# Ten of thirty-six token tiles: the second feed-forward product as seven half products a pair, joint row statistics, buffers by number, and a new order of all steps

## The chip, the cores and the metric

The kernel runs on one core of a Trainium2 chip. The metric is the device time of one launch in microseconds (us). The core has TensorE (PE in the profile, its weight loads PEld), VectorE (DVE), ScalarE (ACT), GpSimd (POOL) and SyncE (SP), which issues every transfer here.

## The reference

Linear attention, eight batches of eight heads over 576 positions of 64 values, followed by a feed-forward block with a normalised SoLU:

```
q_s = softmax(q, over the 64 values)      k_s = softmax(k, over the 576 positions)
kv  = k_s^T v          (64 x 64 for each head)
x   = q_s kv           -> 4608 tokens x 512
h   = x @ w_in         -> 4608 x 1024
sm  = softmax(h);  solu = h * sm
ln  = (solu - mean) / sqrt(var + 1e-6) * g_ln
out = ln @ w_out       -> 4608 x 512
```

Everything is float32 in and out; the feed-forward weights arrive as float64 words.

## The kernel before, in words

The 4608 tokens are 36 tiles of 128: four (batch, c) tiles for each batch, and one tile for the 64 left-over rows of each two batches. Tiles are numbered 0 to 35 in the order of the batches; 26 and 34 are the left-over tiles of batches 4/5 and 6/7.

A float32 product is made on TensorE from float16 halves: each operand is split into a high and a low part, and high times high, low times high and high times low are summed, three 128-deep matmuls where one would do. The first four tiles use float32 matmuls instead (L775), since the split weights aren't ready yet.

For a tile the steps are: keys and queries softmax (`keys`, `queries`), attention (`attend`, L645), the first product h = x w_in (L783, 24 matmuls 512 wide), the row statistics and the split `u` of the SoLU value (`hidden`, L791 to L854), a transposing transfer of `u` into `uT` (L831), and the second product (`project`, L872): 24 matmuls with 512 columns of moving weights `wo`, stationary operand `uT`, into one PSUM bank. The last tile (35) has its product in two column halves, 24 matmuls 256 wide each. Then ScalarE or VectorE multiplies by the row factor (L885, L883) and SP stores the rows (L888).

From batch 3 on the first product is made for tiles in pairs (`hidden_twin`, L713): two tiles times the two halves of the contraction times two halves of the columns is a 2 x 2 block product, done with seven half products instead of eight, from sums and differences of blocks (`combined` for x, `weights_combined`, step T, for the weights). The statistics of each tile still run by themselves in `hidden`: row maximum, exponential with its sum (L797), the power on GpSimd for the reciprocal (L807), the SoLU value (L814), mean, split, squares (L836), the power for the root (L854).

Nothing is scheduled at run time. `ORDER` is a string of step names; `in_turns` advances one Python generator for each name, and each `yield` ends a step. The instructions thus go into each engine's queue in exactly this order, and each queue runs in order. A suffix .v puts a step on VectorE instead of its own engine. K, Q, V are the steps of a batch's keys, queries and values, x attention, w and y the input and output weights, W and Z their scaling, h, H, o the hidden steps, paired first products and second products, S and R scales and left-over queries, P four idle matmuls ("warm-up", L935).

Buffers of SBUF come from pools that rotate by tag (`uT` 12, `e` 3, `u` 3, `xT` 3, ...); PSUM has three banks `att`, one bank `o` (the last six tiles use both) and two 2-bank slots `h`.

Of the kernel before, what the change touches and what calls it, by code (L numbers as in the profile page):

```python
# [1002 lines left out]
```

## Time and profile before

| what | value |
|---|---|
| three runs, median (lowest to highest) | 443.63 us (443.26 to 443.71) |
| profiled execution, span first to last instruction | 442.6 us |
| TensorE busy | 422.5 us, 95% |
| VectorE / ScalarE / GpSimd busy | 353.7 / 316.8 / 277.2 us |
| DMA | 73.98 MB, mean 167 GB/s |

The profiled execution's own time is known as its span, 442.6 us; the median of the runs is 1.0 us above it. The shares of busy time are means over stages: the first 60 us load and split the weights and the first keys, the middle has all engines full, and in the last 35 us hardly anything but the second product is left.

### The profile page before, as it was taken

Reading aid. Unit: us, or ns where it says so; the run is one execution under the profiler, and the core shown is the slowest. Engines: PE = TensorE matmul, PEld = TensorE weight load, DVE = VectorE, ACT = ScalarE, POOL = GpSimd, SP = SyncE. Lnnn points to the kernel's source line nnn. Section 1 sums busy time; section 2 is a strip of 40 time slices with the busy share of each in tenths; the row PEclk is TensorE's granted clock in tenths of the full one; section 3 lists DMA queues with packets and bytes.
Section 4 is the critical chain, followed back from the end, with each engine's and each line's share of the span. In section 5 each row is a group of like instructions: output and inputs, shape, how many; then the busy total and the mean of one; then the engine's idle time right before and its main releaser. Section 6 shows DMA issues by size and latency. Waiting matters only on the chain.

```text
span 442.6 us, 8818 instructions
## 1 busy us (share of the span) xinstructions
PE 422.5 (95%) x3285; PEld 202.8 (46%) x3285; DVE 353.7 (80%) x740; ACT 316.8 (72%) x549; POOL 277.2 (63%) x330
## 2 busy tenths in 40 slices
PE   2698899999999999999999999999999999999996
PEld 1443344454454444444544445444454444444444
DVE  5999999999998999969988788897776869554431
ACT  2799998696885768778875667588885869683420
POOL 4206974789998768949966988739854464541220
PEclk9999999999999999999999999999999999999999
DMA  8999788579999786478995658966074481635333
GB/s 276 407 309 318 140 154 229 103 210 202 209 208 213 177 131 138 115 201 216 199 246 126 168 100 215 210 170 145 1 169 77 95 189 22 144 71 118 84 99 81
DMA packets 167083, 73.98 MB, mean 167 GB/s; under 512 B 146424, under 2 KB 155904, under 8 KB 167040
## 3 DMA queue, kind: packets, MB, share of 16 engines
q1 hardware_dynamic: 167040, 73.42, 70.5%
q8 instruction: 26, 0.43, 0.4%
q14 instruction: 17, 0.14, 0.1%
HBM read 36.70 MB, written 9.44 MB: 104 GB/s over the span
## 4 chain that ended last, share of the span: by engine, by line
PE 87%; DVE 7%; ACT 2%; issue 1%; DMA 1%; POOL 1%; DVEq 0%; ACTq 0%
PE o L872 42%; PE h L713 22%; PE h L783 12%; PE kv L450 4%; PE x L645 4%; PE h L775 2%; DMA qm<-in_q_dram 1%; DVE iw L265 1%; DVE top L791 1%; DVE gw L265 1%; PE warm_up L935 1%; ACT wi L292 0%; DVE gw L263 0%; DVE qsum L507 0%; DVE qnmx L500 0%
## 5 line engine op out<-in xcount | busy, mean ns | idle before, releaser
L872 PE MATMUL o<-wo,uT 128*128 128x512 f16 (+1 forms) x888 | 195.3, 373 | 0.0
L872 PEld LDWEIGHTS <-uT 128*128 128x128 f16 x888 | 86.1, 98 | 98.8 <-issue 1.8
L783 PE MATMUL h<-wi,xT 128*128 128x512 f16 x240 | 54.4, 379 | 0.0
L713 PE MATMUL h<-wt,split 128*128 128x512 f16 x198 | 46.0, 379 | 0.0
L885 ACT ACTIVATE os<-o,rr 128x512 f32<-128x512 f32 (+1 forms) x28 | 19.0, 678 | 30.6 <-PE o L872 26.8
L713 PEld LDWEIGHTS <-split 128*128 128x128 f16 x264 | 25.8, 98 | 31.5 <-issue 0.7
L436 POOL TENSOR_TENSOR km<-km,kb 128x1152 f32<-128x1152 f32 x13 | 36.7, 2832 | 4.7 <-ACT kb L414 3.2
L824 POOL TENSOR_TENSOR u<-e,u 128x1024 f16<-128x1024 f32 x12 | 26.3, 2191 | 20.0 <-ACT u L151 14.9
L783 PEld LDWEIGHTS <-xT 128*128 128x128 f16 x240 | 23.0, 98 | 27.6 <-issue 0.6
L797 ACT ACTIVATE e<-h,nm,hs 128x1024 f32<-128x1024 f32 x28 | 33.7, 1202 | 0.7
L854 POOL TENSOR_TENSOR r<-var,mhalf 128x1 f32<-128x1 f32 x36 | 22.3, 621 | 17.7 <-DVE var L846 16.9
L527 POOL TENSOR_TENSOR qhl<-qm,qhl 128x512 f16<-128x512 f32 x24 | 28.1, 1189 | 7.6 <-ACT qhl L151 7.0
L814 DVE SCALAR_TENSOR_TENSOR e<-h,ph,e 128x1024 f32<-128x1024 f32 x22 | 28.1, 1280 | 4.3 <-POOL ph L810 2.8
L807 POOL TENSOR_TENSOR p<-pi,mone 128x1 f32<-128x1 f32 x36 | 22.5, 626 | 14.0 <-DVE pi L804 12.5
L713 PE MATMUL h<-wi,xT 128*128 128x512 f16 x132 | 31.0, 379 | 0.0
L775 PE MATMUL h<-iw,xT 128*128 128x512 f32 x64 | 29.4, 602 | 1.2 <-ACT e L838 1.2
L713 PEld LDWEIGHTS <-xT 128*128 128x128 f16 x198 | 19.0, 98 | 22.7 <-issue 0.6
L502 POOL TENSOR_TENSOR qm<-qm,qnmx 128x1024 f32<-128x1024 f32 (+1 forms) x14 | 25.7, 1839 | 5.7 <-DVE qnmx L500 5.7
L520 POOL TENSOR_TENSOR qm<-qm,qrec 128x1024 f32<-128x1024 f32 x12 | 24.3, 2028 | 7.0 <-DVE qrec L511 6.9
L836 ACT ACTIVATE e<-e 128x1024 f32<-128x1024 f32 x22 | 23.2, 1056 | 3.7 <-DVE u L824 3.6
L801 POOL TENSOR_SCALAR am<-top 128x1 f32<-128x1 f32 x22 | 8.3, 376 | 27.9 <-DVE top L746 12.9
L820 ACT ACTIVATE e<-e,nmu 128x1024 f32<-128x1024 f32 x22 | 25.3, 1149 | 0.3
(209 smaller groups left out, 835.3 us busy)
## 6 DMA issues: line engine op xcount, KB each, us to landing
km<-in_k_dram SPq DMA_DIRECT2D x7, 1152.0 KB, 7.5
vm<-in_v_dram SPq DMA_DIRECT2D x28, 288.0 KB, 4.3
out_dram<-os SPq DMA_DIRECT2D x31, 256.0 KB, 3.0
qm<-in_q_dram SPq DMA_DIRECT2D x7, 1024.0 KB, 6.8
wo<-in_moe_w_in_dram SPq DMA_DIRECT2D x4, 512.0 KB, 9.0
w_in<-in_moe_w_in_dram SPq DMA_DIRECT2D x4, 512.0 KB, 9.3
wo<-in_moe_w_out_dram SPq DMA_DIRECT2D x4, 512.0 KB, 4.3
w_out<-in_moe_w_out_dram SPq DMA_DIRECT2D x4, 512.0 KB, 9.0
```

Source lines behind the costliest of these rows:

```text
L436: on(nc.gpsimd).tensor_tensor(km[:, ns], km[:, ns], wide, op=ALU.subtract)
L502: on(nc.gpsimd).tensor_tensor(x, x, wide(nmx), op=ALU.add)
L520: on(nc.gpsimd).tensor_tensor(x, x, wide(rec), op=ALU.mult)
L527: on(nc.gpsimd).tensor_tensor(lo, y, hi, op=ALU.subtract)
L713: nc.tensor.matmul(out, lefts[left](s, i), right_block(right, r, i), start=(n == 0 and not onto), stop=(n + 1 == len(terms)), skip_group_c ...
L775: nc.tensor.matmul(h[:, ns], xT[:, kc], iw[kc][:, ns], start=(i == 0), stop=(i == NP - 1))
L783: nc.tensor.matmul(h[:, ns], xT[:, t, kc], wi[:, s, kc, ns], start=(i == 0), stop=(i == len(terms) - 1))
L797: nc.scalar.activation(e, h, AF.Exp, bias=nm, scale=hs, accum_out=z)
L814: nc.vector.scalar_tensor_tensor(y, h, ph, e, op0=ALU.mult, op1=ALU.mult, accum_out=s1)
L820: nc.scalar.activation(e, e, AF.Identity, bias=nmu)
L824: on(nc.gpsimd).tensor_tensor(u[:, 1], e, u[:, 0], op=ALU.subtract)
L872: nc.tensor.matmul(o, uT[:, j, f], wo[:, s, f, cols], start=(f == 0 and j == 0 and s == 0), stop=(f == NF - 1 and j == 1))
```

## The change

1. **Second product in seven half products.** For the five tile pairs in `SPLIT_OUT` (27 with 28, 29 with 30, 31 with 32, 33 with 35, 26 with 34; ten tiles) `project` is replaced. Two tiles (rows) by two halves of the 1024 contraction by two halves of the 512 output columns is the same 2 x 2 scheme as in `hidden_twin`. Step U (`hidden_pair`, `split_pair`) forms the sums of the SoLU values and splits them in four parts a, b, c, d, each with its own transposing transfer (three of 2048, one of 1024 columns); step O (`pair_products`) has seven products of 12 matmuls, 256 columns wide, into three PSUM banks x, y, z; step E (`pair_rows`) combines, scales and stores. The weights' sums and differences are made once in step TO (`out_combined`): twelve additions or subtractions on GpSimd or VectorE, four casts on ScalarE.
2. **Joint statistics.** The two tiles of such a pair have their statistics in two columns of one small tile, so each small step runs once a pair; both tiles wait for the maxima of both.
3. **Fixed places.** SBUF buffers of 4 KB a partition are 25 numbered "page" places, PSUM is four "bank" and two "h" places; which buffer gets which place stands in a table, `SLOTS`.
4. **Scales.** The normalisation's constants are folded into the scale columns (`isc` has four), so one small step falls away in the single tiles; the reciprocal may run on VectorE.
5. **Order.** The whole `ORDER` string is new, from the first load on. The number of warm-up steps stays seven (28 matmuls).

```
-BUFS = 12, 3, 2
+BUFS = 25, 2
+SPLIT_OUT = (27, 29, 31, 33, 26)
+SLOTS = {
+    "page": (
+        "0 2 5 1 3 4 6 7 8 9 10 11 12 13 14 15 16 17 18 19 20 21 22 23 24 0 2 3 5 11 12 13 16 17 10 4 20 9 22 21 5 "
...
-    "LQ0 Q0b*3 Q0a P LK0 K0 LQ0 LK0 Q0a V02 V01 Q0b Q0a K0 Q0c V00 V03 Q0b*2 V02 K0 V00 K0*3 V01 Q0a K0 w0 "
+    "LK0*2 P*3 K0 LG K0*5 LQ0 Q0a P*2 K0 Q0a V01 K0*4 LG Q0a V02*2 Q0b Q0b.v LG V00*2 LQ0 K0.v K0 Q0c V03*2 Q0a "
...
+    "U26*2 O33*2 U26*2 E33.v E29 E33 E31*2 O26 o25 O33 E33 E33.v O26*2 E26*4 O26*2 E26 h6 E26 O33 O26 E26*2 E33*3 "
+    "O26 E26*3 h3 "
...
+    def hidden_pair(row_tiles):
...
+        nm = pair("nm2")
+        on(nc.gpsimd).tensor_tensor(nm, tops, col(1), op=ALU.mult)
...
+            nc.scalar.activation(e[i], h[i], AF.Exp, bias=nm[:, i : i + 1], scale=hs, accum_out=z[:, i : i + 1])
...
+        for i in range(2):
+            nc.vector.scalar_tensor_tensor(
+                e[i], h[i], ph[:, i : i + 1], e[i], op0=ALU.mult, op1=ALU.mult, accum_out=nmu[:, i : i + 1]
+            )
...
+    def split_pair(row_tiles, name, e, s2):
...
+            cast(on(nc.scalar), u[:, 0], x)
+            yield
+            on(nc.gpsimd).tensor_tensor(u[:, 1], x, u[:, 0], op=ALU.subtract)
+            yield
+            lefts_of[row_tiles[0], part] = turned(None, u, name, part)
...
+        on(nc.gpsimd).tensor_tensor(sums[:, 0], a21, a22, op=ALU.add)
+        yield
+        on(nc.gpsimd).tensor_tensor(a21, a11, a21, op=ALU.subtract)
...
+    def out_combined():
...
+                x = blocks[i, j] = sb.tile([P, NF // 2, DM // 2], F32, name=f"ob{i}{j}", **place("page", SB))
+                on(nc.gpsimd).tensor_tensor(x, wo[:, 0, rows, cols], wo[:, 1, rows, cols], op=ALU.add)
...
+    def pair_products(row_tiles):
...
+        for acc, left, right in (
+            ("x", "11", "11"), ("y", "s2", "t2"), ("z", "s1", "t1"), ("x", "12", "21"), ("y", "s3", "t3"),
+            ("y", "22", "t4"), ("z", "s4", "22"),
+        ):
...
+            for f in range(NF // 2):
+                for n, (j, s) in enumerate(((0, 0), (1, 0), (0, 1))):
+                    nc.tensor.matmul(
+                        accs[acc], t[:, j, first + f], out_block(right, s, f), start=(f == n == 0 and not onto),
...
+    def pair_rows(row_tiles):
...
+        cast(on(nc.scalar), out_rows[:, 0, left], accs["x"])
+        nc.vector.tensor_tensor(accs["y"], accs["y"], out_rows[:, 0, left], op=ALU.add)
...
+        scaled(1, left, "y")
+        yield
+        stored(1)
+        yield
+        scaled_onto(0)
+        yield
+        stored(0)
```

**The start.** SP's queue before, first rows (`qm` queries, `km` keys, `wi` here the place of the first values, `wo` the words of w_in):

```order
L198 DMA qm_96<-in_q_dram 128x8x128
L228 DMA km_110<-in_k_dram 128x2x576
L198 DMA qm_96<-in_q_dram 128x8x128
L228 DMA km_110<-in_k_dram 128x2x576
L211 DMA wi<-in_v_dram 128x576 x4
L250 DMA wo<-in_moe_w_in_dram 128x1024 x2
```

and after the change:

```order
L250 DMA km_98<-in_k_dram 128x2x576 x2
L351 DMA gl_rows<-in_moe_g_ln_dram 8x128
L220 DMA qm_128<-in_q_dram 128x8x128
L233 DMA wi<-in_v_dram 128x576 x3
L220 DMA qm_128<-in_q_dram 128x8x128
L233 DMA wi<-in_v_dram 128x576
L272 DMA wo<-in_moe_w_in_dram 128x1024 x2
```

Both halves of the keys go first, and the gain vector has moved up to the start; the amount ahead of the weights is the same but for its 4 KB. VectorE's queue before, where the key maxima have just been taken (`col` the turned maxima, `km` minus its maximum, `qn` the normalised queries):

```order
L404 TENSOR_REDUCE col_164<-turned_154 128x4
L153 COPY qT_0_180<-qt_1_134 128x512
L502 TENSOR_TENSOR qm_96<-qm_96,qnmx_2_129 128x8x128
L436 TENSOR_TENSOR km_110<-km_110,kb_173 128x2x576 x2
L507 TENSOR_REDUCE qsum_2_233<-qm_96 128x16
L509 TENSOR_SCALAR qden_2_235<-qsum_2_233 128x16
L511 RECIPROCAL qrec_2_237<-qden_2_235 128x16
L517 TENSOR_TENSOR qn_2_128<-qm_96,qrec_2_237 128x2x4x64
```

and after the change, from the same reduction of the turned maxima on:

```order
L427 TENSOR_REDUCE col_148<-turned_143 128x4
L523 TENSOR_REDUCE qnmx_1_162<-qm_128 128x8
L525 TENSOR_TENSOR qm_128<-qm_128,qnmx_1_162 128x8x64
L356 COPY gl<-turned_gl 128x8
L459 TENSOR_TENSOR km_98<-km_98,kb_155 128x2x576
L523 TENSOR_REDUCE qnmx_2_172<-qm_128 128x16
L530 TENSOR_REDUCE qsum_0_176<-qm_128 128x8
L532 TENSOR_SCALAR qden_0_178<-qsum_0_176 128x8
L534 RECIPROCAL qrec_0_180<-qden_0_178 128x8
L175 COPY vm<-wi 128x9x64
```

One of the two subtractions on the keys has gone to GpSimd, the copy into `qT` to ScalarE and the product `qn` to GpSimd; a copy of values has come. Counted over the whole stretch of VectorE's queue that stands ahead of the first low part of the output weights (L368 before, L391 after): gone are one subtraction on `km`, the copy `qT`, the product `qn`, two of three low parts of `wi` (L294, now later) and two single-column steps; new are one subtraction on half of `qm` (512 wide), one maximum `qnmxr` (512 wide), one copy `vm` (576 wide), one `xT` half (256 wide), two more `bd` (256 wide) and some seven single-column steps. TensorE's queue now begins with twenty warm-up matmuls in a row, ahead of the transposes of the key maxima; before, four stood there.

**The end.** VectorE's queue before, last rows (`e` the SoLU value, `u` its split, `os` the output rows):

```order
L824 TENSOR_TENSOR u_4_5398<-e_4_5347,u_4_5398 128x1024
L883 TENSOR_SCALAR os_20_5470<-o_20_5387,rr_2_5385 128x512
L846 TENSOR_SCALAR var_4_5477<-z_4_5475,s_4_5473 128x1
L883 TENSOR_SCALAR os_40_5530<-o_40_5483,rr_4_5481 128x512
L883 TENSOR_SCALAR os_31_5560<-o_31_5535,rr_3_5455 128x256
```

and after the change (`o_4x`, `o_4y`, `o_4z` the three banks of the pair 26/34):

```order
L1077 TENSOR_SCALAR os_2_5498<-o_2x,rr_2_5496 128x256
L1083 SCALAR_TENSOR_TENSOR os_0_5354<-o_0z,rr_0_5312,os_0_5354 128x256
L1083 SCALAR_TENSOR_TENSOR os_2_5498<-o_2z,rr_2_5496,os_2_5498 128x256
L1077 TENSOR_SCALAR os_2_5498<-o_2y,rr_2_5496 128x256
L1091 TENSOR_TENSOR o_4y<-o_4y,os_4_5623 128x256
L1083 SCALAR_TENSOR_TENSOR os_4_5623<-o_4z,rr_4_5621,os_4_5623 128x256
L1083 SCALAR_TENSOR_TENSOR os_2_5498<-o_2z,rr_2_5496,os_2_5498 128x256
L1083 SCALAR_TENSOR_TENSOR os_4_5623<-o_4z,rr_4_5621,os_4_5623 128x256
```

The last instruction is 256 wide in both. SP's queue ends before with one store of 128 rows by 256 columns behind it; after the change the last pair is that of the left-over tiles, whose rows belong to two batches, and four stores of 64 rows by 512 columns end the queue, two of them behind the last instruction of VectorE.

## Rows read from the trace of the kernel before

**Rows 1.** The profile's page, part 1: busy us, share, instructions by engine.

```profile
PE 422.5 (95%) x3285; PEld 202.8 (46%) x3285; DVE 353.7 (80%) x740; ACT 316.8 (72%) x549; POOL 277.2 (63%) x330
```

**Rows 2.** Windows: length, busy us of PE, PEld, DVE, ACT, POOL; clock, DMA, GB/s.

```profile
0.00:62.60 62.60, 47.29 (x466) 23.95 (x467) 54.97 (x106) 50.78 (x82) 31.56 (x33) 1.00 0.92 277
62.60:340.00 277.40, 276.02 (x2262) 131.51 (x2261) 242.72 (x515) 210.86 (x371) 209.74 (x239) 1.00 0.75 166
340.00:439.10 99.10, 99.07 (x561) 47.39 (x559) 55.49 (x120) 55.15 (x98) 35.91 (x60) 1.00 0.48 105
```

**Rows 3.** Timeline of VectorE, start.

```profile
4.97 1.28 DVE L500 TENSOR_REDUCE qnmx<-qm 128x8 f32<-128x512 f32 x2 [3.97 <-DMA qm<-in_q_dram]
...
10.47 0.68 DVE L425 TENSOR_TENSOR khalf<-km 128x512 f32<-128x512 f32 x1
...
11.98 0.29 DVE L430 TENSOR_TENSOR ktop<-ktop,km 128x128 f32<-128x128 f32 x1
...
13.51 0.68 DVE L153 COPY qT<-qt 128x512 f32<-128x512 f32 x1
...
15.59 2.63 DVE L436 TENSOR_TENSOR km<-km,kb 128x1152 f32<-128x1152 f32 x2
...
19.98 0.69 DVE L517 TENSOR_TENSOR qn<-qm,qrec 128x512 f32<-128x512 f32 x1
...
37.30 2.48 DVE L294 SCALAR_TENSOR_TENSOR wi<-iw,s_in,wi 128x1024 f16<-128x1024 f32 x2
```

**Rows 4.** Chain of waits in order of time: start us, us, what.

```profile
160.61 5.18 PE o L872 x24
...
405.50 33.74 PE o L872 x180
439.27 0.48 DVE os L883
```

**Rows 5.** Timeline of SP, the last stores: start us, issue us.

```profile
439.78 0.34 SPq L888 DMA_DIRECT2D out_dram<-os  x1
```

**Rows 6.** Timeline of PEld, weight loads in the last half product: start us, us.

```profile
434.49 4.46 PEld L872 LDWEIGHTS <-uT 128*128 128x128 f16 x41
```

**Rows 7.** Timeline of VectorE, statistics of a late pair.

```profile
383.01 0.14 DVE L746 DVE_READ_ACCUMULATOR2_ANT top<- 128x1 f32 x1
...
384.57 0.21 DVE L753 TENSOR_SCALAR top<-top,top 128x1 f32<-128x1 f32 x1
...
387.43 1.28 DVE L814 SCALAR_TENSOR_TENSOR e<-h,ph,e 128x1024 f32<-128x1024 f32 x1 [0.92 <-POOL ph L810]
```

**Rows 8.** Line L692, ns min/median/max, first and last start.

```profile
L692 DVE SCALAR_TENSOR_TENSOR sums<-x,xT x11: 411/421/425, 160.2 to 365.4; 128x256 f32<-128x256 f32 x11
```

**Rows 9.** Waits of TensorE: total us, times, longest.

```profile
PE qt L572 <- POOL qn L517: 6.2, 1, 6.2
...
PE kv L450 <- issue: 1.2, 2, 0.7
```

**Rows 10.** Timeline of TensorE, warm-ups of the start.

```profile
1.73 1.89 PE L935 MATMUL warm_up<-bd 128*128 128x512 f16 x4 [1.73 <-POOL bd L134]
...
12.80 1.91 PE L935 MATMUL warm_up<-bd 128*128 128x512 f16 x4
...
32.73 1.03 PE L935 MATMUL warm_up<-bd 128*128 128x512 f16 x4
```

**Rows 11.** Timeline of SP, two stores of 64 rows: start us, issue us.

```profile
435.54 1.10 SPq L888 DMA_DIRECT2D out_dram<-os  x2
```

**Rows 12.** Line L888, all stores, from issue to landing.

```profile
DMA to landing us min/median/max: 1.8/3.0/7.7
```

**Rows 13.** Tile uT, all transposing transfers, from issue to landing.

```profile
DMA to landing us min/median/max: 4.3/4.4/8.3
```

**Rows 14.** Line L824, the split: ns min/median/max, first and last start.

```profile
L824 POOL TENSOR_TENSOR u<-e,u x12: 2125/2132/2850, 203.9 to 394.1; 128x1024 f16<-128x1024 f32 x12
```

**Rows 15.** Line L502, ns min/median/max, first and last start.

```profile
L502 POOL TENSOR_TENSOR qm<-qm,qnmx x14: 1043/1903/2281, 5.7 to 310.3; 128x1024 f32<-128x1024 f32 x12, 128x512 f32<-128x512 f32 x2
```

More of the change, by code (lines that the diff above doesn't have):

```diff
@@ L107, in linear_attention_solu_ffn, with place @@
     QS = 2.0**14
-    US = 2.0**14
+    US = 2.0**12
     EPS_SCALE = 1e6 / US**2
-    UB, XB, WB = BUFS
+    SB, WB = BUFS
+    slots = {kind: iter(places.split()) for kind, places in SLOTS.items()}
+    def place(kind, bufs):
+        return dict(tag=f"{kind}{next(slots[kind])}", bufs=1) if kind in slots else dict(tag=kind, bufs=bufs)
+    ROOT = (EPS_SCALE / DF) ** 0.5
     cst = ctx.enter_context(tc.tile_pool(name="cst", bufs=1))
@@ L283, in weights_in_scaled @@
         yield
-        wide = ps.tile([P, P], F32, name="wide_in", tag="att", bufs=3)
+        wide = ps.tile([P, P], F32, name="wide_in", **place("bank", 4))
         yield from largest(m1, wide, "in")
@@ L398, in tops_of @@
             return
[L399 removed]
+        turned = ps.tile([P, 2, P], F32, name=f"turned{b}", **place("bank", 4))
         for i in range(2):
@@ L408, in tops_of @@
         yield
-        wide = ps.tile([P, 2, P], F32, name=f"wide{b}", tag="att", bufs=3)
+        wide = ps.tile([P, 2, P], F32, name=f"wide{b}", **place("bank", 4))
         for i in range(2):
@@ L422, in keys @@
         top = sb.tile([P, NP, D], F32, name=f"ktop{b}", tag="ktop", bufs=1)
-        half = sb.tile([P, NP, KC // 2, D], F32, name=f"khalf{b}", tag="khalf", bufs=1)
+        half = sb.tile([P, NP, KC // 2, D], F32, name=f"khalf{b}", **place("page", SB))
         for ns in parts if b == 0 else [slice(0, NP)]:
@@ L439, in keys @@
             yield
-        banks = [ps.tile([P, 512], F32, name=f"kv{b}_{r}", tag="att", bufs=3) for r in range(2)]
+        banks = [ps.tile([P, 512], F32, name=f"kv{b}_{r}", **place("bank", 4)) for r in range(2)]
         kv = banks[0]
@@ L562, in whole_queries @@
         if ("whole", first) not in hl_of:
-            hl_of["whole", first] = sb.tile([P, 2, H, D], F32, name=f"qn{b}_{first}", tag="qhl", bufs=1)
+            hl_of["whole", first] = sb.tile([P, 2, H, D], F32, name=f"qn{b}_{first}", **place("page", SB))
         cs = range(c0, c1)
@@ L574, in whole_queries @@
             if (b, c) not in qT_of:
-                t = sb.tile([P, 2, NP, P], F32, name=f"qT{b}_{first}", tag="qT", bufs=2)
+                t = sb.tile([P, 2, NP, P], F32, name=f"qT{b}_{first}", **place("page", SB))
                 qT_of.update({(b, k): t for k in (first, first + 1) if (b, k) in whole})
@@ L619, in attend_whole @@
         yield
-        xT = xT_of[b, c] = sb.tile([P, NP, P], F32, name=f"xT{b}_{c}", tag="xT", bufs=XB)
+        xT = xT_of[b, c] = sb.tile([P, NP, P], F32, name=f"xT{b}_{c}", **place("page", SB))
         for i, acc in enumerate(banks):
@@ L635, in attend @@
             ]
-        flat = [ps.tile([P, 512], F32, name=f"x{name}_{g}", tag="att", bufs=3) for g in range(2)]
+        flat = [ps.tile([P, 512], F32, name=f"x{name}_{g}", **place("bank", 4)) for g in range(2)]
         accs = [t[:, 0 : NP // 2 * n * P].rearrange("p (i c k) -> p i c k", c=n, k=P) for t in flat]
@@ L732, in hidden_twin @@
         yield
-        tops = [sm.tile([P, 1], F32, name=f"top{name}_{i}", tag="ttop", bufs=8) for i in range(4)]
+        tops = [sm.tile([P, 1], F32, name=f"top{name}_{i}", tag="ttop", bufs=8) for i in range(3)]
+        both = sm.tile([P, 2], F32, name=f"tops{name}", tag="tops", bufs=2)
         nc.vector.tensor_tensor_reduce(t1[:, left], t1[:, left], w_, 1.0, -3.0e38, ALU.add, ALU.max, tops[0])
@@ L792, in hidden @@
         nm = sm.tile([P, 1], F32, name=f"nm{name}", tag="nm")
-        nc.scalar.activation(nm, top, AF.Copy, scale=minus if row_tile in done else hs)
+        nc.scalar.activation(nm, top, AF.Copy, scale=scale[:, 1:2] if twin else hs)
         yield
-        e = sb.tile([P, DF], F32, name=f"e{name}", tag="e", bufs=3)
+        e = sb.tile([P, DF], F32, name=f"e{name}", **place("page", SB))
         z = sm.tile([P, 1], F32, name=f"z{name}", tag="z")
@@ L817, in hidden @@
         yield
-        u = sb.tile([P, 2, DF], F16, name=f"u{name}", tag="u", bufs=3)
-        if row_tile in done:
+        u = sb.tile([P, 2, DF], F16, name=f"u{name}", **place("page", SB))
+        if twin:
             nc.scalar.activation(e, e, AF.Identity, bias=nmu)
@@ new lines, in linear_attention_solu_ffn, with inverse2, halves @@
+    rows_of = {}
+    def inverse2(eng, out, x):
+        if eng is nc.vector:
+            eng.reciprocal(out, x)
+        else:
+            eng.tensor_tensor(out, x, mone.broadcast_to([P, 2]), op=ALU.pow)
+    lefts_of = {}
+    HALF = DF // 2
+    def split_pair(row_tiles, name, e, s2):
+        def halves(x, part, n=DF):
+            u = sb.tile([P, 2, n], F16, name=f"u{name}{part}", **place("page", SB))
+            cast(on(nc.scalar), u[:, 0], x)
+            yield
+            on(nc.gpsimd).tensor_tensor(u[:, 1], x, u[:, 0], op=ALU.subtract)
+            yield
+            lefts_of[row_tiles[0], part] = turned(None, u, name, part)
+            yield
+        left, right = slice(0, HALF), slice(HALF, DF)
+        a11, a12, a21, a22 = (x[:, cols] for x in e for cols in (left, right))
+        yield from halves(e[0], "a")
+        junk = sb.tile([P, DF], F32, name=f"junk{name}", **place("page", SB))
+        for i in range(2):
+            nc.scalar.activation(junk, e[i], AF.Square, accum_out=s2[:, i : i + 1])
+            yield
+        sums = sb.tile([P, 2, HALF], F32, name=f"su{name}", **place("page", SB))
+        on(nc.gpsimd).tensor_tensor(sums[:, 0], a21, a22, op=ALU.add)
+        yield
+        on(nc.gpsimd).tensor_tensor(a21, a11, a21, op=ALU.subtract)
+        yield
+        on(nc.gpsimd).tensor_tensor(sums[:, 1], sums[:, 0], a11, op=ALU.subtract)
+        yield
+        on(nc.gpsimd).tensor_tensor(a12, a12, sums[:, 1], op=ALU.subtract)
+        yield
+        yield from halves(e[1], "b")
+        yield from halves(sums.rearrange("p i f -> p (i f)"), "c")
+        yield from halves(a12, "d", HALF)
@@ new lines, in pair_rows, with scaled, scaled_onto, stored @@
+    def pair_rows(row_tiles):
+        name = name_of(row_tiles[0])
+        rr = sm.tile([P, 2], F32, name=f"rr2{name}", tag="rr2", bufs=3)
+        on(nc.gpsimd).tensor_tensor(rr, rows_of[row_tiles[0]], osc.broadcast_to([P, 2]), op=ALU.mult)
+        yield
+        accs = acc_of[row_tiles[0]]
+        left, right = slice(0, DM // 2), slice(DM // 2, DM)
+        out_rows = sb.tile([P, 2, DM], F32, name=f"os{name}", **place("page", SB))
+        def scaled(i, cols, k):
+            eng, acc = on(nc.scalar), accs[k]
+            if eng is nc.vector:
+                eng.tensor_scalar(out_rows[:, i, cols], acc, rr[:, i : i + 1], None, op0=ALU.mult)
+            else:
+                eng.activation(out_rows[:, i, cols], acc, AF.Copy, scale=rr[:, i : i + 1])
+        def scaled_onto(i):
+            o = out_rows[:, i, right]
+            nc.vector.scalar_tensor_tensor(o, accs["z"], rr[:, i : i + 1], o, op0=ALU.mult, op1=ALU.add)
+        def stored(i):
+            for rows, dst in destinations(row_tiles[i]):
+                nc.sync.dma_start(out=dst, in_=out_rows[rows, i])
+        cast(on(nc.scalar), out_rows[:, 0, left], accs["x"])
+        yield
+        nc.vector.tensor_tensor(accs["y"], accs["y"], out_rows[:, 0, left], op=ALU.add)
+        yield
+        scaled(0, right, "y")
+        yield
+        scaled(0, left, "x")
+        yield
+        scaled(1, right, "y")
+        yield
+        scaled_onto(1)
+        yield
+        scaled(1, left, "y")
+        yield
+        stored(1)
+        yield
+        scaled_onto(0)
+        yield
+        stored(0)
+        yield
@@ L867, in project @@
             w = cols.stop - cols.start
-            o_tag = "att" if t >= LATE and (t + i) % 2 else "o"
-            o = ps.tile([P, w], F32, name=f"o{name}{i}", tag=o_tag, bufs=3 if o_tag == "att" else 1)
+            o = ps.tile([P, w], F32, name=f"o{name}{i}", **place("bank", 4))
             for f in range(NF):
@@ L879, in project @@
             else:
-                part = sb.tile([P, DF], F32, name=f"os{name}{i}", tag="e", bufs=3)[:, 0:w]
+                part = sb.tile([P, DF], F32, name=f"os{name}{i}", **place("page", SB))[:, 0:w]
             eng = on(nc.scalar)
```

241 lines of the change are left out of this document (176 added, 65 removed), and 113 rows, old and new, of tables (ORDER, SLOTS).

## Prediction

> **What bounds the kernel now.** I read the page's engine shares first, then windows by stage, then the chain of waits, then single engines. TensorE is busy 422.5 of 442.6 us and nobody else comes near [rows 1]. The windows show that this share is made of two unlike stages [rows 2]. From 62.6 us on TensorE is busy 276.02 of 277.40 and 99.07 of 99.10 us: 1.41 us idle in 376.5. There, only less work on TensorE shortens anything. Before 62.6 us it is busy 47.29 us and VectorE 54.97; of VectorE's 7.63 idle us, 4.97 lie ahead of its first row [rows 3]. So the start is bounded by the first transfers and VectorE's queue. Then comes a tail: the last product ends, VectorE works 0.48 us, a store is issued at 439.78, and the span ends at 442.6 [rows 4, 5]. The granted clock reads 1.00 in all three windows [rows 2].
>
> **Term 1, the products: -5.9 us.** The chain gives 5.18 us for 24 matmuls 512 wide, 0.2158 each [rows 4]. Its 180 in 33.74 us are 132 of these, 28.49 us, and the last tile's 48 of 256 columns in the other 5.25, or 0.1094 each: half the columns cost half the time, with 0.0015 us on top. The five pairs lose 216 x 0.2158 + 48 x 0.1094 = 51.86 us and gain 5 x 84 x 0.1094 = 45.95. What could spoil it is the weight load: a 256-wide matmul gives it only 0.109 us of cover. The half product of before does just that, with 41 loads recorded in 4.46 us, 0.109 apiece, at the pace of the matmuls [rows 6], so I take them as hidden.
>
> [...]
>
> **Term 2, the start: -1.5 us.** Ahead of the first low part of the output weights VectorE loses half of 2.63 (a subtraction on `km`), 0.68 (`qT`), 0.69 (`qn`), 2.48 (two low parts of `wi`), all in rows 3, and two small steps at some 0.14 [rows 7]: 5.4 us. New are a 512-wide subtraction by the `qn` row, 0.69; a maximum, half of 1.28, 0.64; a 576-wide copy by the `qT` row, 0.77; three 256-wide ones at 0.42 [rows 8], 1.26; seven small ones at 0.14, 1.0: 4.4 us. The queue is shorter by 1.0. With the keys first the key maxima no longer stand behind those of the queries (two reductions of 1.28 from 4.97 [rows 3]), and TensorE's 6.2 us wait for `qn` [rows 9] should mostly go. I add 0.5 for that, out of the 2.7 us that VectorE idles after its first row. Bounds: -3.7 if all 2.7 go. On the other side stand the twenty warm-ups. [...] One half of the keys takes 1.80 us from its first maximum to its last, 10.47 to 12.27 [rows 3], so two halves from 4.97 are done near 8.6. [...]
>
> **Term 3, the tail: +0.9 us.** The last VectorE operation, 0.42 for 256 columns [rows 8], stands in place of 0.48. Behind it go two stores of 64 rows, issued in 1.10 us together [rows 11], in place of one in 0.34 [rows 5]: +0.7; and half of a second 0.42 us operation, as the last product now feeds two rows. Lower bound +0.2, when one store is issued already (0.55 less 0.34). Upper bound +2.0, when landing also takes the median 3.0 us instead of the least, 1.8 [rows 12].
>
> **Term 4, new waits of TensorE: +0.8 us.** The order is new everywhere, and the trace can't show how its waits fall. Lower bound 0. Nearest rows: 1.41 us in all over 376.5 us [rows 2], single waits up to 0.7 [rows 9]. The pairs are more tightly bound: seven products share three banks, four transposing transfers of 4.4 us (at most 8.3) a pair stand ahead of them where two stood [rows 13], and behind a late one every matmul of TensorE's queue stands. I put the upper bound at 4, five pairs at 0.8, and take 0.8, near the row.
>
> **At no cost: the helpers' extra work.** GpSimd has 18 more operations of 1024 elements, 12 of them step TO's; at 2.13 [rows 14] 38.4 us, and 11 of 512 at 1.04 [rows 15], 11.4 us: 50 us. Its free time is 67.7 us in the middle and 63.2 in the end [rows 2]. VectorE has 14 more of 512 and 24 of 256 elements, at 0.69 [rows 3] and 0.42 [rows 8] 9.7 + 10.1 = 20 us, with 34.7 and 43.6 us free. DMA moves ten more transposing transfers and stands at 0.75 and 0.48. If cover is missing, it comes up in term 4. The constants folded into the scales and small steps joined by pair lie off TensorE's path.
>
> GpSimd's split takes 2132 ns in the median and 2850 at most, 0.7 us more in single cases [rows 14]. [...] All 29 new GpSimd operations at +0.7 would be 20 us, which its free time still holds.
>
> **Sum.** -5.9 - 1.5 + 0.9 + 0.8 = -5.7: a span of 436.9 from 442.6. The median of the runs is 1.0 above the span, so 437.9.
>
> **Rivals.**
> 1. *The products alone.* The start gives nothing, since its end is set by the weights' transfers (DMA is at 0.92 and 277 GB/s there [rows 2], and the bytes ahead are the same), and new waits cost 2.5. For it: that share. Against it: VectorE is the fuller one. -5.9 + 0.9 + 2.5 = -2.5: 441.1.
> 2. *All falls into place.* Start -3.7, no waits, tail +0.2: -9.4, 434.2. For it: 15.3 us of idle TensorE in the start. Against: twenty warm-ups ahead of the key maxima.
> 3. *Slower: joint statistics hold the first product's two slots.* Both `h` slots now wait for the later tile's maximum: 383.15 to 384.78 in a pair of before, 1.63 us, with the SoLU value at 387.43 [rows 7]. The next paired first product needs them. If nothing else is queued for TensorE then, five pairs cost 5 x 1.63 = 8.1 us: -5.7 + 8.1 = +2.4, 446.0. It decides from 1.1 us uncovered a pair on (5.7 / 5). Against it: a second product of 9.2 us (84 x 0.1094) can be put between, and after the last pairs no first product follows.
> 4. *Slower: every weight load is bare.* 420 loads of 0.109 in place of 264 would add 156 x 0.109 = 17.0 us: +11.3, 454.9. Rows 6 speak against it.
>
> **Chances.** Forecast 0.64, rival 1 0.18, rival 2 0.09, rival 3 0.07, rival 4 0.02. The forecast's own range is 435.2 to 439.8. The whole range, 434.0 to 442.4, takes in rivals 1 and 2 and leaves out 3 and 4 and the worst of 1. What a measurement can tell from no change is 0.2%, 0.9 us. Faster: 0.64 + 0.09 and 0.14 of rival 1, 0.87; no change: the other 0.04 of rival 1; slower: 0.09.
>
> **What would show it.** Right: TensorE busy about 416.6 us; 420 matmuls of 256 columns in the pair products at 0.109 each; TensorE idle under 3 us from its filling to the last product; the transposes of the key maxima at 8.6 to 10.3 us and the first low part of the output weights a microsecond or two earlier; two 64-row stores of 0.55 each behind VectorE's last row. Wrong: TensorE idle over 5 us after the start, above all on an `h` slot ahead of a paired first product (rival 3) or on transposed parts between 340 and 430 us (term 4); a pitch above 0.12 (rival 4); a stage before the first output weights as long as it was (rival 1); or the higher clock level reached later than the 32.7 us at which rows 10 show it.

## The result, and the profile after

The changed kernel takes 447.34 us in the median of 4 runs (447.21 to 447.61), the kernel before 443.56 (443.26 to 443.71): a ratio of 1.009, with an interval of 1.0075 to 1.0104. It is slower by 0.9%. The forecast was 437.9 with a range of 434.0 to 442.4; both the sign and the range are wrong.

The page of the kernel after, parts 1 and 2, answers to [rows 1]. The second line is the granted clock in 40 slices.

```profile
PE 420.4 (94%) x3441; PEld 219.0 (49%) x3441; DVE 383.4 (86%) x783; ACT 323.0 (72%) x555; POOL 307.1 (69%) x305
...
PEclk9969999999999999999999999999999999999999
```

Windows of the kernel after, with the columns of [rows 2]; the first three answer to its rows (the last is longer here, up to the last product), then parts of the middle, then three small ones.

```profile
0.00:62.60 62.60, 50.38 (x468) 24.90 (x468) 53.44 (x107) 48.87 (x80) 33.67 (x31) 0.95 0.97 286
62.60:340.00 277.40, 268.90 (x2222) 128.05 (x2223) 250.70 (x515) 209.43 (x369) 212.31 (x210) 1.00 0.73 164
340.00:441.40 101.40, 101.17 (x752) 66.08 (x750) 78.80 (x163) 64.68 (x109) 61.11 (x66) 1.00 0.70 139
...
62.60:280.00 217.40, 208.90 (x1788) 99.78 (x1789) 196.11 (x401) 167.29 (x298) 169.64 (x164) 1.00 0.74 166
280.00:340.00 60.00, 60.00 (x436) 28.27 (x434) 54.59 (x115) 42.14 (x73) 42.67 (x47) 1.00 0.68 154
...
59.00:280.00 221.00, 211.79 (x1795) 100.73 (x1794) 199.64 (x408) 170.68 (x304) 172.87 (x168) 1.00 0.74 166
...
20.00:24.00 4.00, 2.16 (x38) 1.46 (x28) 3.93 (x8) 3.01 (x4) 2.35 (x2) 1.00 1.03 394
24.00:28.00 4.00, 3.20 (x9) 1.92 (x8) 3.93 (x8) 3.89 (x9) 0.94 (x1) 0.53 1.04 402
28.00:32.00 4.00, 4.00 (x21) 1.61 (x20) 3.90 (x6) 3.13 (x8) 0.00 (x0) 0.62 1.02 376
```

Windows of the kernel before, of stretches that are compared with these.

```profile
62.60:280.00 217.40, 216.02 (x1827) 103.23 (x1826) 193.88 (x403) 163.96 (x290) 170.25 (x191) 1.00 0.81 180
...
59.00:280.00 221.00, 219.19 (x1835) 104.55 (x1834) 196.70 (x414) 167.12 (x296) 173.57 (x196) 1.00 0.81 180
...
20.00:24.00 4.00, 2.86 (x86) 2.08 (x78) 3.80 (x10) 3.40 (x6) 1.57 (x1) 1.00 0.98 356
24.00:28.00 4.00, 4.00 (x12) 1.75 (x12) 4.00 (x6) 3.97 (x8) 0.00 (x0) 1.00 0.74 254
```

The time can be booked on TensorE, whose last product ends at 441.37 us, 2.1 later than the 439.27 of before [rows 4]:

| | before | after | difference |
|---|---|---|---|
| TensorE busy | 422.5 | 420.4 | -2.1 |
| TensorE idle, 0 to 62.6 us | 15.31 | 12.22 | -3.1 |
| idle, 62.6 to 340 us | 1.38 | 8.50 | +7.1 |
| idle, 340 us to the last product | 0.03 | 0.23 | +0.2 |
| behind the last product | 3.33 | 4.43 | +1.1 |

Idle is window less busy. Two rows matter. The middle lost 7.1 us, all of it before 280 us: from 280 to 340 TensorE is busy 60.00 of 60.00. (The joint statistics of the new pairs begin only at 338.9 us, their products at 376.7.) One wait of 1.47 us, from 61.9 to 63.4, straddles the edge at 62.6; counted from 59 us on, so that it is in whole, the idle time up to 280 us rose from 1.8 to 9.2 us, by 7.4. And busy time fell by 2.1 instead of 5.9, mostly because the start alone is busy 3.1 us longer (50.38 against 47.29 [rows 2]), at a clock of 0.95. Between 24 and 32 us the clock reads 0.53 and 0.62, after a window in which TensorE was busy 2.16 of 4 us; the kernel before, busy 2.86 there, keeps 1.00. The timeline of TensorE after shows what that costs, and the warm-ups ahead of it.

```profile
1.73 7.16 PE L1186 MATMUL warm_up<-bd 128*128 128x512 f16 x20 [1.73 <-POOL bd L156]
8.72 0.38 PE L424 MATMUL turned<-ident,ktop 128*128 128x128 f32 x2
...
10.73 1.90 PE L1186 MATMUL warm_up<-bd 128*128 128x512 f16 x8
...
23.54 0.66 PE L595 MATMUL qt<-ident,qn 128*128 128x128 f32 x4 [1.27 <-POOL qn L540]
...
25.90 3.62 PE L817 MATMUL h<-iw,xT 128*128 128x512 f32 x4
...
30.51 3.95 PE L817 MATMUL h<-iw,xT 128*128 128x512 f32 x8
```

Four first products take 3.62 us at 25.90, eight take 3.95 at 30.51: 0.905 against 0.494 each; the clock reads 0.50 from 25.9 to 29.5 us and 0.93 from 30.5 to 34.4. Eight warm-ups at 10.73 take 1.90, 0.24 each, where four took 1.91 at 12.80 before, 0.48 each [rows 10]; the clock column reads 1.00 in both places (8 to 12 us after, 12 to 16 before). So the faster pace comes earlier, and is lost again.

The waits of TensorE after, 62.6 to 436 us (total us, times, longest), answer to [rows 9].

```profile
PE h L741 <- DVE top L773: 1.5, 1, 1.5
PE wide_out L192 <- DVE m_out L377: 1.5, 1, 1.5
PE h L825 <- ACT e L879: 1.3, 2, 0.8
PE kv L473 <- issue: 1.2, 1, 1.2
PE h L741 <- ACT vw L173: 0.8, 1, 0.8
```

They are single waits of about a microsecond, most on VectorE or ScalarE. One shows how they can come about. TensorE of after:

```profile
244.54 1.46 PE L741 MATMUL h<-wi,split 128*128 128x512 f16 x6
247.48 1.46 PE L741 MATMUL h<-wt,xT 128*128 128x512 f16 x6 [1.48 <-DVE top L773]
```

VectorE of after, the same moment:

```profile
244.51 0.79 DVE L620 TENSOR_TENSOR hs<-inv_kv,isc 128x4 f32<-128x4 f32 x1
245.22 0.41 DVE L720 SCALAR_TENSOR_TENSOR sums<-x,xT 128x256 f32<-128x256 f32 x1
245.55 1.21 DVE L448 TENSOR_TENSOR khalf<-km 128x1024 f32<-128x1024 f32 x1
246.69 0.69 DVE L773 CUSTOM_DVE_ANT_0 h<-h,vw 128x512 f32<-128x512 f32 x1
```

The row-maximum step at 246.69 has to read the bank before TensorE's next product adds to it. It stands behind a key-maximum step of the next batch (the 1.21 us row); VectorE works without a gap while TensorE waits 1.48 us for it. The product of the same kind before, on VectorE:

```profile
237.10 0.70 DVE L744 CUSTOM_DVE_ANT_0 h<-h,vw 128x512 f32<-128x512 f32 x1 [0.88 <-PE h L713]
```

There VectorE waits 0.88 us for TensorE, not the other way round.

The end of the chain after, answering to [rows 4], and one of the new products (ns min/median/max), answering to [rows 6]:

```profile
440.02 1.32 PE o_4z L1058 x12
441.34 0.03 issue
441.37 0.48 DVE os L1083
```

```profile
L1058 PE MATMUL o_0x<-wo,uT_0a x48: 269/272/273, 376.7 to 418.6; 128*128 128x256 f16 x48
```

Twelve half products take 1.32 us, 0.110 each. (The 272 ns are each one's length; they overlap.)

### The profile page after: what moved, and what is told of

Read it like the earlier page. It is cut to its first block, busy times and chain, and to the rows that moved or that the text cites. A ratio compares the mean times of both kernels' runs of the same rounds, so it can differ in the third digit from the quotient of the medians.

```text
span 445.8 us, 9199 instructions
## 1 busy us (share of the span) xinstructions
PE 420.4 (94%) x3441; PEld 219.0 (49%) x3441; DVE 383.4 (86%) x783; ACT 323.0 (72%) x555; POOL 307.1 (69%) x305
## 5 line engine op out<-in xcount | busy, mean ns | idle before, releaser
L1122 PE MATMUL o<-wo,uT 128*128 128x512 f16 x624 | 141.2, 379 | 0.3 <-DVE wo L391 0.3
L1122 PEld LDWEIGHTS <-uT 128*128 128x128 f16 x624 | 60.2, 98 | 72.4 <-issue 2.2
L525 POOL TENSOR_TENSOR qm<-qm,qnmx 128x1024 f32<-128x1024 f32 (+1 forms) x13 | 23.8, 1838 | 14.6 <-DVE qnmx L523 14.5
L473 PE MATMUL kv<-vm,km 64*64 64x65 f32 x1152 | 20.2, 220 | 5.1 <-ACT km L461 2.9
L840 ACT ACTIVATE e<-h,nm,hs 128x1024 f32<-128x1024 f32 x20 | 24.0, 1202 | 0.4
L173 ACT COPY vw<-h 128x512 f32<-128x512 f32 x26 | 14.9, 584 | 12.2 <-DVE top L763 9.1
L473 PEld LDWEIGHTS kv<-vm,km 64*64 64x64 f32 x1152 | 18.4, 134 | 9.5 <-ACT km L461 4.1
L730 POOL TENSOR_TENSOR split<-sums,split 128x1024 f16<-128x1024 f32 x9 | 19.7, 2187 | 1.4 <-ACT split L173 1.3
L530 DVE TENSOR_REDUCE qsum<-qm 128x16 f32<-128x1024 f32 (+1 forms) x17 | 19.5, 1149 | 1.2 <-ACT qm L527 1.2
L523 DVE TENSOR_REDUCE qnmx<-qm 128x16 f32<-128x1024 f32 (+1 forms) x17 | 19.5, 1150 | 0.9 <-DMA qm<-in_q_dram 0.9
L857 DVE SCALAR_TENSOR_TENSOR h<-h,ph,e 128x1024 f32<-128x1024 f32 x14 | 18.0, 1287 | 2.1 <-POOL ph L853 1.6
## 6 DMA issues: line engine op xcount, KB each, us to landing
w_in<-in_moe_w_in_dram SPq DMA_DIRECT2D x4, 512.0 KB, 10.3
```

Source lines behind the costliest of these rows:

```text
L473: nc.tensor.matmul(o, km[half, n, c], vm[half, n, c], start=(m == 0 and c == 0), stop=(m == 1 and c == KC - 1))
L525: on(nc.gpsimd).tensor_tensor(x, x, wide(nmx), op=ALU.add)
L730: on(nc.gpsimd).tensor_tensor(split[:, 1], sums, split[:, 0], op=ALU.subtract)
L840: nc.scalar.activation(e, h, AF.Exp, bias=nm, scale=hs, accum_out=z)
L1122: nc.tensor.matmul(o, uT[:, j, f], wo[:, s, f, cols], start=(f == 0 and j == 0 and s == 0), stop=(f == NF - 1 and j == 1))
```

## The experiments

Eleven variants ran: some on the kernel after, some on the kernel before. The kernel before, run again beside them, had medians between 443.37 and 443.53 us. Ratios are to before; differences to the kernel after (447.34) are differences of medians. "Idle" below is TensorE's in 62.6 to 280 us, from each one's window; in x_clock, x_dve, x_clockdve and x_best the wait that straddles 62.6 lies wholly ahead of it, which makes some 0.8 us of a difference.

**The clock alone (x_clock).** 21 matmuls that nobody reads stand in TensorE's gaps between 12 and 25 us.

```
+    def keep_busy(acc, n):
+        for _ in range(n): ... nc.tensor.matmul(acc, i[:, 0:P], i[:, 0 : acc.shape[1]], start=True, stop=True)
...
+        keep_busy(kv, 4 if b == 0 else 0)
...
-            turned = ps.tile(...)
+            turned = ps.tile(...); keep_busy(..., {2: 4, 3: 3}.get(c, 0))
...
-        qT, kvn = qT_of[b, c][:, c % 2], kvn_of[b]
+        qT, kvn = ...; keep_busy(..., {0: 6, 1: 4}.get(c, 0))
```

> The changed kernel with 21 more idle matmuls (no other edit) in TensorE's gaps between 13 and 25 us: 4 ahead of the first key product, 6 and 4 of 256 columns ahead of the first two attention products, 4 and 3 ahead of two transposes of queries. They keep TensorE busy where, in the changed kernel, it was busy about half the time before its clock fell at 24.5 us until 31. Theory A (the lost clock costs what TensorE did in those 6.5 us at half speed): granted clock 1.00 throughout, the four float32 matmuls that took 3.62 us take 1.9, and the time falls by 2.7 to 3.8 us, to 443.5 to 444.6. Theory B (the loss sits in VectorE's fuller queue from 62 to 280 us, and the start is covered by it): the clock stays up but the time falls by 1 us at most, 446.3 or more.

Measured: 444.87 us (444.32 to 445.23), ratio 1.0028 (1.0018 to 1.0039). Its windows:

```profile
62.60:280.00 217.40, 210.69 (x1797) 100.06 (x1796) 197.96 (x398) 168.26 (x297) 170.95 (x164) 1.00 0.76 169
...
20.00:24.00 4.00, 3.18 (x40) 2.13 (x33) 3.91 (x8) 2.79 (x4) 2.47 (x2) 1.00 1.02 399
24.00:28.00 4.00, 4.00 (x31) 2.05 (x30) 3.96 (x6) 3.96 (x9) 0.82 (x1) 1.00 1.04 402
```

With 3.18 us of work in place of 2.16 ahead of it, the clock stays at 1.00, and its first four products take 1.88 us instead of 3.62. That is worth 2.5 us, a little less than theory A's 2.7 to 3.8: the fall of the clock is one cause of the loss. Over its eight runs the mean granted clock is 0.993 to 1.000, over the four of the kernel after 0.987 to 0.992. The middle is still 6.7 us idle, 8.2 from 59 us on.

**Fewer warm-ups (x_p1).** Four in place of the twenty at the start.

```
-            for _ in range(4):
+            for _ in range(0 if 1 < len(warmed) < 6 else 4):
```

> The changed kernel with 4 idle matmuls in place of 20 at its start (the four later warm-up steps of the first five issue nothing). Theory A1 (TensorE's half-empty stretch from 12.6 to 24 us is what lowers the clock): the clock is then low up to 25 us or later just the same, the float32 matmuls around 26 to 31 us run at the low level, and the time stays within 0.8 us of the changed kernel's 447.3. Theory A2 (the early rise itself is spent and so costs: without it the level rises once, near 16 us as in the kernel before, and stays): no low stretch after 20 us and 445.3 or less.

Measured: 448.94 us (447.92 to 449.51), ratio 1.012 (1.0101 to 1.014), 1.6 more than the kernel after. Windows:

```profile
24.00:28.00 4.00, 3.20 (x10) 1.84 (x8) 3.93 (x8) 3.92 (x9) 0.98 (x1) 0.57 1.06 404
...
56.00:62.60 6.60, 6.60 (x15) 2.72 (x14) 6.32 (x18) 6.27 (x14) 6.01 (x8) 0.81 0.87 157
```

The clock falls at 24 us again and once more ahead of 62.6. The twenty are thus no loss, and A2 falls; but the time lies outside A1's bounds too. They cost nothing ahead of the products: the key maxima's transposes start at 8.33 here and at 8.72 in the kernel after, and both reach the first transposes of the queries within 0.1 us of each other.

**GpSimd's new step TO left out (x_noto).** Twelve additions or subtractions and four casts are not made; the products read other weights in their place.

```
-                on(nc.gpsimd).tensor_tensor(x, wo[:, 0, rows, cols], wo[:, 1, rows, cols], op=ALU.add)
+                pass
...
-            return ot[name][:, s, f]
+            name = {"t1": "12", "t2": "21", "t3": "22", "t4": "11"}[name]
```

> The changed kernel without the work of step TO: the twelve additions and subtractions and the four casts that make the combined output weights are left out, and plain blocks of the output weights are used in their place (the output is another). All other steps and their order stay. Theory A (clock at the start): the same time within 0.5 us, 446.8 to 447.8. Theory B (the middle is too full): GpSimd is relieved of 24 us, VectorE of 2.5 and ScalarE of 3 between 94 and 270 us; TensorE's 8.7 us of waits after 62.6 us shrink by 1 to 3 us and the time falls to 444.3 to 446.3.

Measured: 445.61 us (444.98 to 445.75), ratio 1.0043 (1.0028 to 1.0058): 1.7 less than the kernel after, inside theory B. Window, and a row of TensorE's timeline:

```profile
62.60:280.00 217.40, 212.01 (x1800) 100.85 (x1801) 194.49 (x398) 166.48 (x297) 146.26 (x155) 0.99 0.75 168
...
177.51 4.44 PE L741 MATMUL h<-wi,xT 128*128 128x512 f16 x12 [2.10 <-ACT e L879]
```

GpSimd's 23.4 us in this window were priced at nothing; taking them away gives back 3.1 us of idle TensorE there and 1.7 in the time. The time gives back less, as here the clock falls a second time (0.99 over 150 to 280 us, where the kernel after has 1.00), behind a wait of 2.10 us: the twelve products at 177.51 take 4.44 us, those of the kernel after 2.82. One of the additions (1.85 us) and one of the casts (0.69) ran on VectorE, three casts on ScalarE, so this is the price of the whole step and not of GpSimd's queue alone.

**Less work on VectorE, in both orders (x_dve on the kernel after, b_dve on before).** The first two steps of the key maximum are left out in batches 2 to 7, so that the maximum there is taken over three of nine groups: 12.4 us of VectorE by the steps' usual length. In the pages VectorE's busy time falls by 11.5 us on the kernel after and 11.6 on before, and GpSimd's by 5.4 and 6.5.

```
-            nc.vector.tensor_tensor(half[:, ns], km[:, ns, 0 : KC // 2], ...)
+            if b < 2: nc.vector.tensor_tensor(half[:, ns], km[:, ns, 0 : KC // 2], ...)
...
-            nc.vector.tensor_tensor(half[:, ns, 0:2], half[:, ns, 0:2], half[:, ns, 2:4], op=ALU.max)
+            if b < 2: nc.vector.tensor_tensor(half[:, ns, 0:2], ...)
...
```

> The changed kernel with 12.4 us less work on VectorE between 80 and 320 us: in batches 2 to 7 the first two steps of the key maximum (1.28 and 0.79 us) are left out, so the maximum is over three of the nine position groups. Theory B (VectorE, 92 to 95 % busy from 62 to 250 us, has become a second bound and each delay of its queue is TensorE's): TensorE's waits after 62.6 us fall from 8.7 to 5 or less, the time by 3 to 5 us, to 442.3 to 444.3. Theory A: within 0.7 us of 447.3.

> The kernel before with the same work left out on VectorE (first two steps of the key maximum in batches 2 to 7), as control. Both theories: TensorE is the bound there with 1.4 us of waits in 376, so the time stays within 0.6 us of 443.6. If it falls by 2 us or more, less VectorE work helps any order and x_dve says nothing about the new one.

Measured: on the kernel after 442.75 us (442.12 to 445.13), ratio 0.9988 (0.9974 to 1.0001), 4.6 less; on before 443.17, ratio 0.9991 (0.9981 to 1.0001), 0.3 less. The window of the first, then of the second:

```profile
62.60:280.00 217.40, 212.18 (x1808) 101.21 (x1807) 189.40 (x389) 169.10 (x299) 167.39 (x164) 1.00 0.78 170
```

```profile
62.60:280.00 217.40, 216.63 (x1830) 103.61 (x1829) 185.51 (x394) 163.84 (x290) 165.63 (x191) 1.00 0.82 179
```

The same edit is worth 4.6 us in the new order and nothing clear of noise in the old one (part of it may be the clock, which in the profiled run reads 0.60 from 24 to 28 us and 1.00 from 28 to 32, against 0.53 and 0.62 in the kernel after). So TensorE waits there for VectorE's work, though VectorE is idle for 21.3 us of this window in the kernel after; in the kernel before, taking the same work away frees nothing.

**The products alone (b_prod).** On the kernel before, the last ten tiles' second products are made of 420 matmuls of 256 columns, by leaving out the last of the eight slices of the hidden width; order and helpers stay.

```
-                for j, s in ((0, 0), (0, 1), (1, 0)):
+                for j, s in ((0, 0), (0, 1), (1, 0)) if t < 26 or f + 1 < NF else ():
+                    for m in (slice(0, w),) if t < 26 or w < DM else (slice(0, w // 2), slice(w // 2, w)):
```

> The kernel before, its order and all its other work as they are, but the second product of the last ten tiles made with 420 matmuls of 256 columns (42 a tile) in place of 216 of 512 and 48 of 256; the last sixteenth of the contraction of these tiles is left out and nothing is combined, so their output is another. It asks what the cheaper products alone are worth where no order changes. Theory of the prediction: 51.9 less 45.9 us of TensorE in a stage without waits, 5.9 us less, 437.6 (437.0 to 438.4). Rival (256-wide matmuls cost more than half of 512-wide ones, or a second engine takes over at the end): a gain under 4 us, 439.6 or more.

Measured: 438.16 us (437.91 to 438.91), ratio 0.9883 (0.9868 to 0.9897): 5.3 us less. So the first term exists, loads and all. Its profiled run, the slowest of the four, shows that in the order before the clock can fall too, here to 0.57 behind a window in which TensorE was busy 2.86 of 4 us, as in the kernel before; over the whole run it reads 0.996, in the other three 1.00:

```profile
24.00:28.00 4.00, 4.00 (x6) 1.70 (x7) 4.00 (x7) 3.95 (x8) 0.00 (x0) 0.57 0.71 246
```

**Both causes taken away (x_clockdve).** The edits of x_clock and x_dve together, with the same part of the key maximum left out.

> The changed kernel with both x_clock's 21 idle matmuls and x_dve's 12.4 us less VectorE work (the key maximum over three of nine groups in batches 2 to 7). If clock and VectorE are two separate causes, the gains add: 2.5 of the one and 3.5 to 4.6 of the other, 440.2 to 441.4, below the kernel before. If they are one and the same delay seen twice (an earlier start only moves TensorE's waits): 442.3 or more.

Measured: 441.04 us (440.93 to 441.23), ratio 0.9946 (0.993 to 0.9963). It beats both kernels, but with that shorter maximum. Window:

```profile
62.60:280.00 217.40, 214.11 (x1816) 101.85 (x1815) 192.06 (x396) 171.34 (x302) 169.50 (x166) 1.00 0.76 174
```

That is 6.3 us below the kernel after. The two edits by themselves gave 2.5 and 4.6, together 7.1; so they are two causes and not one delay seen twice, but some 0.8 us are counted in both. What remains is 3.3 us idle, 4.8 from 59 us on.

**Seven steps moved and one put on VectorE (x_best, and x_bestdve with the shorter maximum).** On x_clock, steps are exchanged where TensorE waits, and the buffers numbered anew; two of them:

```
-  ... x15*2 Q4a K4*3 V53 ... h13 K4 o10 o10.v ...
+  ... x15*2 Q4a K4 o10 K4*2 V53 ... h13 K4 o10.v ...
-  ... O26 E26*2 E33*3 O26 E26*3 h3
+  ... O26 E26*3 E33*3 O26 E26*2 h3
```

> x_clock with a handful of steps moved by 3 to 70 places in the order, and buffers numbered anew for it: two key steps and one copy of x at the start, one key step of batch 1, one second-product step of tile 10 moved ahead of a key step near 180 us, one step of x31 and one of the last pair's rows. Output as the reference. Theory (TensorE's waits up to 280 us come from the places of a few steps in VectorE's queue): 1 to 2.5 us below x_clock's 444.9, 442.4 to 443.9. Rival (the waits are spread over every step, and moving single ones only moves the wait): within 0.6 us of 444.9.

> x_best with x_dve's 12.4 us less work on VectorE (the key maximum over three of nine groups in batches 2 to 7). By the sum of what was measured for x_clockdve (441.0) and the 1 to 2.5 us expected of x_best: 438.5 to 440.0, the fastest so far. If VectorE's load and the moved steps are the same delay: 440.6 to 441.4.

Measured: x_best 447.14 us (446.5 to 447.52), ratio 1.0079 (1.0067 to 1.0092), 2.3 more than x_clock; x_bestdve 442.03 (441.61 to 442.94), ratio 0.9967 (0.9955 to 0.9979), 1.0 more than x_clockdve; both lie outside the theory's bounds and the rival's. In both, the moved step `x31` reads its queries ahead of their transfer, so the rows made from it are others. In x_bestdve the clock fell as well, to 0.92 over 40 to 62.6 us (x_best 1.00): twelve first products at 55.49 took 7.11 us, in x_best 5.42. The window of x_best:

```profile
62.60:280.00 217.40, 210.13 (x1796) 100.13 (x1796) 197.52 (x397) 168.10 (x297) 171.09 (x164) 1.00 0.75 168
```

7.3 us idle instead of x_clock's 6.7: together these steps took no idle time away. At one place a wait has only moved: ahead of 55.6 us x_clock has two, of 1.47 and 0.60 us, and x_best a single one of 2.38. The change to the last steps probably cost something at the end, as SP's last stores show, of x_best and of x_clock:

```profile
438.85 3.47 SPq L1087 DMA_DIRECT2D out_dram<-os  x6
```

```profile
436.65 3.73 SPq L1087 DMA_DIRECT2D out_dram<-os  x5
```

Six stores from 438.85 on instead of five from 436.65; behind the last product x_best takes 5.7 us, x_clock 4.4.

**More work on VectorE, in both orders (x_more, b_more).** The two key-maximum steps are made twice in batches 2 to 7.

```
-            nc.vector.tensor_tensor(half[:, ns], ...)
+            for _ in range(1 + (b > 1)): nc.vector.tensor_tensor(half[:, ns], ...)
...
```

> The changed kernel with 12.4 us more work on VectorE: the same two steps of the key maximum that x_dve left out are made twice in batches 2 to 7 (the output stays). Theory (in the new order VectorE's queue is on the path from 62 to 280 us): 3 to 6 us slower than the changed kernel, 450.3 to 453.3. Rival (x_dve's gain was only the shorter low-clock stretch of those runs): within 1.5 us of 447.3.

> The kernel before with the same 12.4 us more work on VectorE. Theory (its order leaves VectorE room, though VectorE is as busy there: 193.9 of 217.4 us against 196.1): at most 2 us slower than 443.5. Rival (both orders stand on the same edge, and the difference is load alone): 4 us slower or more, as in x_more.

Measured: on the kernel after 461.89 us (460.55 to 462.29), ratio 1.0403 (1.0377 to 1.0429), 14.5 more; on before 460.49 (458.34 to 462.63), ratio 1.038 (1.0339 to 1.0422), 17 more. The theories had said 3 to 6 more and at most 2 more. Windows, x_more first, then a line of b_more's page:

```profile
62.60:280.00 217.40, 199.61 (x1600) 94.04 (x1600) 197.22 (x377) 155.16 (x277) 161.43 (x152) 0.99 0.69 159
```

```profile
62.60:280.00 217.40, 208.31 (x1774) 98.70 (x1773) 200.78 (x388) 155.68 (x278) 168.86 (x185) 0.99 0.75 165
...
PE 425.9 (93%) x3285; PEld 203.5 (45%) x3285; DVE 372.9 (82%) x752; ACT 317.0 (69%) x549; POOL 285.2 (62%) x330
```

My theory that the order before leaves VectorE room falls. There the two steps left out are worth 0.3 us and the two steps made twice cost 17. The second edit was the larger one, though: twelve more VectorE operations, 12.4 us by their usual length, raised VectorE's busy time by 19.2 us (from 353.7) and GpSimd's by 8.0 (from 277.2); in x_more it was 14.8 and 3.4. TensorE's busy time rose too, by 3.4 us in b_more and 4.3 in x_more, as its clock fell for part of the time (0.99 over 62.6 to 280 us in both; 0.92 over the first 62.6 us of x_more, where the kernel after has 0.95). So both orders stand near the point from which helpers' work shows in the time, and the new one is past it; that is a reading of four edits, not a measured curve.

## Why the prediction was wrong

The span was forecast to fall by 5.7 us and rose by 3.2, so 8.9 us are missing. Booked on the prediction's terms, 6.5 of them are new waits (7.3 where 0.8 stood), 1.5 the start (nothing gained), 0.7 the products and 0.2 the tail.

**Term 1, right.** 0.110 us a half product [rows 4, 6], and 5.3 us less in b_prod, against 5.9 forecast.

**Term 3, right.** +1.1 against +0.9.

**"At no cost: the helpers' extra work", the step that failed, and with it term 4's upper bound of 4.** The prediction set VectorE's 20 us against the 34.7 it is idle in [rows 2], and GpSimd's 50 against 67.7. The sizes were off (both engines' busy time rose by some 30 us, 29.7 and 29.9), but that is not the main point, since most of VectorE's rise lies behind 280 us, where TensorE waits for next to nothing (0.23 us). TensorE's new idle time lies before 280 us, and there VectorE and GpSimd are busy about as long as before (196.1 and 193.9; 169.6 and 170.3). What changed is how much VectorE does for each microsecond of TensorE work. Part of that came with the order: between 62.6 and 280 us VectorE makes three low parts of `wi` where it made one (2.4 us more; two were taken out of the start, a gain that term 2 counted) and three key subtractions where it made one (3.1 us more). The ratio in 62.6 to 280 us, each worked out from its window, with TensorE's idle time there and from 59 to 280 us (ratio and idle time are not independent, so this orders the cases and proves nothing by itself):

| | VectorE / TensorE busy | TensorE idle, us | idle from 59 us, us |
|---|---|---|---|
| b_dve | 0.86 | 0.8 | 0.8 |
| before | 0.90 | 1.4 | 1.8 |
| x_clockdve | 0.90 | 3.3 | 4.8 |
| x_dve | 0.89 | 5.2 | 6.7 |
| x_noto | 0.92 | 5.4 | 6.3 |
| x_clock | 0.94 | 6.7 | 8.2 |
| after | 0.94 | 8.5 | 9.2 |
| b_more | 0.96 | 9.1 | 9.3 |
| x_more | 0.99 | 17.8 | 17.8 |

Idle time of VectorE was no slack: it idles where TensorE hasn't yet filled a bank (the 0.88 us at 237.10 of before), and at other moments its queue is what TensorE waits for (the 1.48 us at 247.48 of after). Less work on VectorE (x_dve) and step TO left out (x_noto) each give back 2.5 to 3 of the 7.4 us; the edits also change how long the other helper is busy (GpSimd 5.4 us less in x_dve), so the runs show that the helpers' work costs TensorE this time, and not how it divides between the two engines. The term's bound took five pairs at 0.8, and the pairs wait for next to nothing (0.23 us from 340 us on); the price was paid by the tiles ahead of them. At equal ratios of 0.9 the new order still idles 3 to 5 us more than the one before. That rest may belong to the places of the steps; no run shows it, and the one attempt at moving them didn't settle it.

**Term 2, wrong in its result.** TensorE's idle time of the start fell by 3.1 us; its wait for `qn` went from 6.2 us [rows 9] to single ones of at most 1.3; the transposes behind the twenty warm-ups stand at 8.72, inside the 8.6 to 10.3. The 10.3 counts all twenty warm-ups at 0.43 us, which no run shows: the twenty take 7.16 us, 0.36 each. But its busy time rose by the same 3.1, and the sign that the prediction named did not come: the first low part of the output weights starts 1.2 us later, not one or two earlier (before, then after; ns min/median/max, first and last start).

```profile
L368 DVE SCALAR_TENSOR_TENSOR wo<-gw,gs,wo x8: 745/745/751, 64.9 to 70.6; 128x512 f16<-128x512 f32 x8
```

```profile
L391 DVE SCALAR_TENSOR_TENSOR wo<-gw,gs,wo x8: 745/748/748, 66.1 to 70.7; 128x512 f16<-128x512 f32 x8
```

What was missing is the clock. The prediction took the 1.00 of before [rows 2] for granted; the shorter waits came as a row of gaps (TensorE busy 2.16 of 4 us from 20 to 24 us), and the clock fell behind them, to 0.53, for 2.5 us in the time. Even where it stays up, in x_clock, that first low part starts at 64.9, as before: VectorE's queue got no shorter by the 1.0 us worked out, and why stays open.

**Rivals.** Rival 1, the products alone, had the direction of the loss (new waits 2.5) but a third of its size. Rivals 3 and 4 fall: there is no wait on an `h` slot from 280 us on, and the joint statistics begin only at 338.9; and with all its loads a half product takes 0.110 us. That rival 3's 446.0 comes nearest to the measured 447.34 is luck. The slower case that came, the helpers' queues over the middle up to 280 us, was not among them.

**Open.** Whether an order exists that keeps the whole of b_prod's 5.3 us with the complete key maximum, why x_p1's clock falls twice, and what VectorE's and GpSimd's queues each cost, wasn't settled.
